# One stream of 64 KiB rows for the key, value and weight tiles of the first attention layer's groups 0 to 5

## The chip, the cores and the metric

The kernel runs on one core of a Trainium2 chip. The metric is the device time of one launch in microseconds (us); less is better. A profile of one execution by the hardware profiler stands beside the times.

## What is computed

One token passes through two layers, each an attention over a cached sequence and then a dense block; both layers use the same weights and the same cache. D is 512, there are 32 heads of 128, 4096 cached keys and a hidden width of 1376. All is float32.

```python
def _A_ref(x, k_cache, v_cache, wq, wo):
    q = (x @ wq).reshape(B, Sq, H, Dh).transpose(0, 2, 1, 3)
    scores = einsum("bhqd,bhkd->bhqk", q, k_cache) * (Dh ** -0.5)
    o = einsum("bhqk,bhkd->bhqd", softmax(scores), v_cache)
    return o.transpose(0, 2, 1, 3).reshape(B, Sq, H * Dh) @ wo

def _B_ref(x, w1, b1, w2, b2):
    return gelu(x @ w1 + b1) @ w2 + b2

for _ in range(2):
    x = x + _A_ref(_layernorm(x), ...)
    x = x + _B_ref(_layernorm(x), ...)
```

The key and value caches are 67 MB each and are read twice.

## The kernel before

The 32 heads are worked on as 8 groups (G) of 4. A group has a K tile and a V tile of 128 partitions x 64 KiB (8.39 MB, `BLOCK`), each made of 8 chunks (`NC`, 1.05 MB, 8 KiB per partition; one chunk holds 512 keys of four heads), and the group's parts of `wq` and `wo`, one chunk each. Layer 0 takes the groups in the order 0 to 7, layer 1 from 7 to 0. All tiles lie in one large tile, `arena`; SyncE issues every load on its one queue (L87, `load`), in program order, and holds an issue until the place it writes has been read by everyone.

In groups 0 to 5 of layer 0 the K tile and the V tile are loaded whole, each in one transfer, into a ring of three places of 64 KiB (`k_home`, `v_home`). The group's `wo` chunk and the next group's `wq` chunk come as a pair in one transfer of 16 KiB rows into a place of their own (`PAIR`). The order on the queue is K, V, pair, next K, and so on.

A group runs like this. `scores` (L232) multiplies each K chunk with the query on TensorE, 8 matmul records a chunk. `softmax` makes the weights `pt`. In a group with `pairs` the V chunks are weighted in place, four by ScalarE (`weighted_by_act`, L269, 16 instructions a chunk) and four by VectorE (`weighted`, L274); `add_pair` (L279) adds two neighbouring chunks to two others, three times, and one last addition (L572) adds the two that are left. With `PAIRS[0]` = (0, 2, 4, 6) the first sum is into chunks 0 and 1. After the first `add_pair`, `queries` (L213 to L223) makes the next group's query from `wq` on VectorE and one TensorE matmul (L217), with the second `add_pair` between; the third and the last addition follow. `sum_over_keys` (L283, TensorE) of the one chunk left, `scaled_out` (L287 to L292) and `summed_wo` (L309, L311), the product with `wo`, are held back (`late_sum`, `late_out`) and run within the next group's scores, after chunk 4.

Group 6 uses matmuls for its V tile (`values`, L262), group 7 gets its tiles in smaller transfers, and then the dense block and layer 1 follow.

Of the kernel before, what the change touches and what calls it, by code (L numbers as in the profile page):

```python
# [14 lines left out]
ALU = mybir.AluOpType  # L15
AX = mybir.AxisListType

P = 128
# [3 lines left out]
G = 8  # L22
J = 4
C = 8
# [3 lines left out]
U = 512  # L28
KEPT = 6

NC = 4 * U
BLOCK = 8 * NC
# [13 lines left out]
PITCH = 1024  # L46
# [7 lines left out]
LAST_IDLE = {3: 1, 5: 1, 6: 1}  # L54
WHOLE, HALVES = ((0, 8),), ((0, 4), (4, 8))
VAR_AT = 1
PAIRS = (0, 2, 4, 6), ((4, 6, 0, 2), (2, 0, 4, 6))


@with_exitstack  # L60
def decode_layers(ctx: ExitStack, tc: tile.TileContext, k, v, w, w1, w2, out):
    nc = tc.nc
    const = ctx.enter_context(tc.tile_pool(name="const", bufs=1))
    work = ctx.enter_context(tc.tile_pool(name="work", bufs=1))
# [20 lines left out]
    def load(at, src):  # L85
        t = arena[:, at : at + src.shape[-1]]
        tc.keep_in_program_order(nc.sync.dma_start(t, src))  # L87
        return t

    def pin(ins):  # L90
        tc.keep_in_program_order(ins)

    def chunk(t, i=0):
        return t[:, NC * i : NC * (i + 1)].rearrange("p (j n) -> p j n", j=4)
# [35 lines left out]
    row, _ = wq_at(0)  # L130
# [11 lines left out]
    pS, pO, pB = (psum.tile([P, 512], F32, name=n) for n in ("pS", "pO", "pB"))  # L142
# [68 lines left out]
    def queries(n, xc, wt, at, t=None, short=False, between=None):  # L211
        t = wt[:, 0, :] if t is None else t
        pin(nc.vector.tensor_scalar(t, wt[:, 0, :], xc[:, 0:1], None, op0=ALU.mult))  # L213
        for c in range(1, 4):
            pin(nc.vector.scalar_tensor_tensor(t, wt[:, c, :], xc[:, c : c + 1], t, op0=ALU.mult, op1=ALU.add))  # L215
        if short:
            pin(nc.tensor.matmul(at, one.to_broadcast([P, P]), t, start=True, stop=True))  # L217
            if between is not None:
                between()
            own = t.rearrange("p (j d) -> p j d", j=J)  # L220
            pin(nc.vector.tensor_tensor(own, at.rearrange("p (j d) -> p j d", j=J),
                                        ident[:, None, :].to_broadcast([P, J, P]), op=ALU.mult))
            pin(nc.vector.tensor_reduce(zq[:, :, C - 1], own, axis=AX.X, op=ALU.add))  # L223
            return zq
        for j in range(J):
            nc.tensor.matmul(at[:, j : j + 1], t[:, P * j : P * (j + 1)], one, start=True, stop=True)
        nc.vector.tensor_copy(zq[:, :, C - 1], at[:, :J])
        return zq
# [36 lines left out]
    def weighted_by_act(pt, t, c):  # L265
        for b in range(4):
            for j in range(J):
                own = by_head(t)[:, j, b]
                nc.scalar.activation(own, own, AF.Copy, scale=pt[:, j, c, b : b + 1])  # L269

    def weighted(pt, t, c):
        own = t.rearrange("p b (j d) -> p b j d", j=J)
        weight = pt[:, :, c, :].rearrange("p j b -> p b j")[:, :, :, None].to_broadcast([P, 4, J, DH])
        nc.vector.tensor_tensor(own, own, weight, op=ALU.mult)  # L274

    def add_pair(at, to, by):

# [3 lines left out]
    def sum_over_keys(t):  # L281
        for j in range(J):
            pin(nc.tensor.matmul(pO[32 * j : 32 * j + 4, :], one.to_broadcast([P, 4]), by_head(t)[:, j],  # L283
                                 start=True, stop=True))

    def scaled_out(rl, ot):
        nc.vector.transpose(ot[:, :512], pO)  # L287
        diag = ot.rearrange("p (b q) -> p b q", q=129)[:, :, :P]
        diag = diag.rearrange("p b (d q) -> p d b q", q=32)[:, :, :, 0]
        o, on = small("o", 4), small("on", 4)  # L290
        nc.vector.tensor_reduce(o, diag, axis=AX.X, op=ALU.add)
        nc.vector.tensor_scalar(on, o, rl, None, op0=ALU.mult)  # L292
        return on
# [14 lines left out]
    def summed_wo(on, wt, t):  # L308
        pin(nc.vector.tensor_scalar(t, wt[:, 0, :], on[:, 0:1], None, op0=ALU.mult))  # L309
        for d in range(1, 4):  # L310
            pin(nc.vector.scalar_tensor_tensor(t, wt[:, d, :], on[:, d : d + 1], t, op0=ALU.mult, op1=ALU.add))  # L311
        return t

    def add_out(t, n):
        pin(nc.tensor.matmul(pB[0:1, :], one, t, start=n == 0, stop=n == G - 2))  # L315
# [104 lines left out]
    xs, s = set_x(ahead[:, X_AT : X_AT + 4], 0.0, ahead[:, X_AT : X_AT + 4])  # L420
    nc.gpsimd.tensor_copy(b1c, ahead[:, B1_AT : B1_AT + FB])
    nc.gpsimd.tensor_copy(b2c, ahead[:, B2_AT : B2_AT + 4])
    here = {}

    def stream(what, g, pieces, base):

        for a, b in pieces:
            t = load(base + NC * a, part(k if what == "k" else v, g, a, b))
            for c in range(a, b):
                here[what, g, c] = chunk(t, c - a)  # L430
                yield c, here[what, g, c]

    w1_t = arena[:, HELD:PAIR]
    w2_t = [[arena[:, at : at + U] for at in homes] for homes in W2_AT]

# [3 lines left out]
    for layer in range(2):  # L439
        order = list(range(G)) if layer == 0 else list(range(G))[::-1]  # L440
        if layer == 0:
            nm, ss, xc = mean_of(xs, s, pN[:, 0:1], True)
            z = queries(0, xc, wq_first, pO)
        else:
            for c in range(4):
                query_block(c, xs, wq_first)
                if c == 1:
                    nm, ss, xc = mean_of(xs, s, pN[:, 0:1])
        if layer == 1:
# [5 lines left out]
            z = first_queries(negm)  # L455
        xc_l = small("xc_l", 4)
        r = rstd_of(ss, pN[:, 1:2], True)
# [4 lines left out]
        late = None  # L462
        for n, g in enumerate(order):
            first, final = n == 0, n == G - 1
            pairs = None
            if layer == 0 and n < G - 2:
                pairs = PAIRS[0]
            if layer == 1 and 1 < n < G - 2:
                pairs = PAIRS[1][n % 2]

            k_home, v_home = ((2 * n + i) % 3 * BLOCK for i in (1, 2))
            if layer == 1:
                k_home, v_home = K2_HOME if n == 2 else 15 * NC, 6 * NC * (n % 2)

            if layer == 1 and n == 0:
                tiles = [(c, here["k", g, c]) for c in range(C)]
            elif layer == 1 and n == 1:
                tiles = [(c, here["k", g, c]) for c in range(2)]
                tiles += list(stream("k", g, ((2, 3), (3, 4), (4, 8)), -2 * NC))
                n_kept = STAY + U * KEPT  # L480
                load(V1_HOME[6] + n_kept % NC, v[g][:, n_kept:BLOCK])
                for u in range(STAY, n_kept - U, U):
                    nc.scalar.copy(v_next(u), pK[(u - STAY) // U])
                for c in range(STAY // NC, C):
                    here["v", g, c] = chunk(arena[:, V1_HOME[c] : V1_HOME[c] + NC])
            elif layer == 1 and n == 2:
                tiles = [(c, here["k", g, c]) for c in range(6)]
                tiles += list(stream("k", g, ((6, 8),), 2 * BLOCK - 6 * NC))
            else:
                tiles = stream("k", g, HALVES if final else WHOLE, k_home)  # L490
            for c, t in tiles:
                scores(z, c, t)
                if late is not None and c == 4:
                    late[0]()
            held = late is not None
            if held:
                late[1]()
                late = None
# [3 lines left out]
            p, ot = free_now(layer, n)  # L502
            if layer == 1 and first:
                z = queries(n + 1, xc_l, wq_next, pO)
                nc.scalar.copy(v_next(STAY + U * KEPT - U), pB)
            pt, rl = softmax(sc, nsc, p, held)
# [3 lines left out]
            if layer == 1 and n == 0:  # L510
                for c in range(C):
                    values(c, pt, here["v", g, c], c)
            elif layer == 1 and n == 1:
                for c in range(C):
                    values(c, pt, here["v", g, c], c)

                for _ in stream("k", order[2], ((0, 6),), K2_HOME):
                    pass
            elif final:
                last_v = chunk(arena[:, v_home + BLOCK - NC : v_home + BLOCK])  # L520
                for _ in range(FILL - 2 + layer):
                    idle(t, pS)
                for c, t in stream("v", g, LAST, v_home):
                    values(c, pt, t, c, C - 1)
                    if c == C - 2:
                        others = scaled_out(rl, ot)
                    for _ in range(LAST_IDLE.get(c, 0)):
                        idle(t, pS)
                for a, b in END_PARTS[layer]:
                    at = BLOCK - NC + U * a  # L530
                    load(v_home + at, v[g][:, at : BLOCK - NC + U * b])
                for c in range(C):
                    here["v", g, c] = chunk(arena[:, v_home + NC * c : v_home + NC * (c + 1)])
            else:
                for c, t in stream("v", g, WHOLE, v_home):
                    for i in range(KEPT - 1):
                        if layer == 0 and n == G - 2 and c == (STAY + U * i) // NC:
                            nc.scalar.copy(pK[i], t[:, STAY // U % J + i - J * (c - STAY // NC), :])
                    if pairs is None:
                        values(c, pt, t, c)  # L540
# [23 lines left out]
            else:  # L564
                t = load(PAIR, of_w(wo_at(g) if layer == 0 else wq_at(g - 1), 2))
                wo_t, wq_next = (chunk(t, i) for i in ((0, 1) if layer == 0 else (1, 0)))
            if pairs:
# [6 lines left out]
                def late_sum(rl=rl, ot=ot, wt=wo_t, total=total):  # L574
                    sum_over_keys(total)
                    summed_wo(scaled_out(rl, ot), wt, ot[:, :U])

                def late_out(ot=ot, n=n):
                    add_out(ot[:, :U], n)
# [106 lines left out]
```

## Time and profile before

| what | us |
|---|---|
| median of 3 runs | 673.24 (673.19 to 673.25) |
| the profiled execution | 673.77 |
| its span, first to last instruction | 672.0 |
| VectorE busy | 406.7 |
| TensorE matmul busy | 301.1 |
| ScalarE busy | 215.4 |

The span has 6011 instructions, and 285.36 MB were moved at 425 GB/s on the mean. Busy times of different engines overlap. K0 stands for the K tile of group 0, V0 for its V tile, and so on. A DMA record is counted where a packet ends, so a window of few microseconds can show a DMA share above 1.

### The profile page before, as it was taken

The page shows a single profiled execution, that of the slowest core. Times are in us where ns is not written, and L with a number is a line of the kernel's source. Part 1 is how long each engine was busy: PE and PEld are TensorE (multiplying, and loading weights), DVE is VectorE, ACT ScalarE, POOL GpSimd, SP SyncE. Part 2 cuts the span into 40 slices and gives each one's busy share as a digit, 9 for nine tenths or more (in the row PEclk, how much of TensorE's full clock was granted, in tenths as well). Part 3 has the DMA queues.
Part 4 walks back from the last instruction along what each step waited for, and adds up shares of the span by engine and source line. Part 5 has one row for each costly group of instructions (what it writes and reads, how often), then busy time and mean ns, then how long its engine had stood idle before and what let it go on. Part 6 is the DMA issues. An engine that isn't in the chain of part 4 may idle for free.

```text
span 672.0 us, 6011 instructions
## 1 busy us (share of the span) xinstructions
PE 301.1 (45%) x2236; PEld 79.4 (12%) x2236; DVE 406.7 (61%) x510; ACT 215.4 (32%) x697; POOL 5.2 (1%) x26
## 2 busy tenths in 40 slices
PE   1501603416016053166698985604316026065597
PEld 1100100101001010011124311101001001011124
DVE  3059679497795876971422313289597794982513
ACT  0047064190560823801011200073290650910010
POOL 1000000000000000000000000000000000000000
PEclk9965855856758557586699998755757758566799
DMA  9999999999999999999999999999999999999997
GB/s 384 429 437 437 438 433 437 410 458 433 437 437 402 466 418 430 421 437 422 429 413 398 391 434 449 426 433 437 421 434 425 433 430 415 456 429 418 429 416 301
DMA packets 11548, 285.36 MB, mean 425 GB/s; under 512 B 1280, under 2 KB 1408, under 8 KB 3840
## 3 DMA queue, kind: packets, MB, share of 16 engines
q1 hardware_dynamic: 11520, 284.99, 99.1%
q8 instruction: 17, 0.28, 0.2%
q14 instruction: 11, 0.09, 0.0%
HBM read 284.92 MB, written 0.07 MB: 424 GB/s over the span
## 4 chain that ended last, share of the span: by engine, by line
DMA 65%; PE 16%; DVE 15%; issue 1%; another core or an unknown queue 1%; SPq 0%; ACT 0%; DVEq 0%; ACTq 0%
DMA arena<-in_v 38%; DMA arena<-in_k 19%; DMA arena<-in_w 8%; PE pS L232 7%; DVE arena L274 7%; PE pO L262 5%; DVE arena L279 3%; DVE arena L311 2%; DVE arena L287 1%; PE pO L283 1%; DVE arena L215 1%; PE pB L323 1%; SPq L87 0%; DVE arena L309 0%
## 5 line engine op out<-in xcount | busy, mean ns | idle before, releaser
L269 ACT ACTIVATE arena<-arena,pt 128x128 f32<-128x128 f32 x640 | 188.0, 387 | 49.1 <-DMA arena<-in_v 45.3
L232 PE MATMUL pS<-arena,smalls 128*8 128x512 f32 x1024 | 147.3, 728 | 78.6 <-DMA arena<-in_k 74.5
L279 DVE TENSOR_TENSOR arena<-arena 128x4096 f32<-128x4096 f32 x30 | 132.6, 4420 | 0.3
L217 PE MATMUL pS<-arena,smalls 128*128 128x512 f32 x20 | 20.7, 1140 | 203.4 <-DVE arena L215 203.4
L274 DVE TENSOR_TENSOR arena<-arena,pt 128x2048 f32<-128x2048 f32 x40 | 89.0, 2286 | 37.3 <-DMA arena<-in_v 34.6
L244 ACT ACTIVATE arena<-pS,smalls 128x512 f32<-128x512 f32 x16 | 12.4, 777 | 292.8 <-DVE smalls L243 292.8
L287 DVE STREAM_TRANSPOSE arena<-pO 128x512 f32<-128x512 f32 x16 | 11.5, 717 | 98.3 <-PE pO L262 60.9
L232 PEld LDWEIGHTS pS<-arena,smalls 128*8 128x8 f32 x1024 | 29.8, 102 | 199.1 <-issue 178.6
L262 PE MATMUL pO<-arena,pt 128*4 128x512 f32 x368 | 46.8, 653 | 10.8 <-DMA arena<-in_v 10.0
L236 DVE TENSOR_REDUCE smalls<-pS 128x1 f32<-128x512 f32 x16 | 11.0, 687 | 62.7 <-PE pS L232 62.7
L215 DVE SCALAR_TENSOR_TENSOR arena<-arena,smalls 128x512 f32<-128x512 f32 x45 | 33.8, 752 | 1.6
L311 DVE SCALAR_TENSOR_TENSOR arena<-arena,smalls 128x512 f32<-128x512 f32 x39 | 29.3, 752 | 1.4
L217 PEld LDWEIGHTS pS<-arena,smalls 128*128 128x128 f32 x20 | 5.0, 312 | 206.1 <-DVE arena L215 206.1
L315 PE MATMUL pB<-arena,smalls 128*1 128x512 f32 x26 | 14.1, 625 | 29.8 <-DVE arena L311 29.8
L246 PE MATMUL pO<-ident,arena 128*128 128x128 f32 x64 | 12.2, 320 | 25.6 <-ACT arena L244 25.2
L572 DVE TENSOR_TENSOR arena<-arena 128x2048 f32<-128x2048 f32 x10 | 22.9, 2292 | 0.3
L262 PEld LDWEIGHTS pO<-arena,pt 128*4 128x4 f32 x368 | 10.0, 92 | 44.4 <-issue 37.5
L382 ACT ACTIVATE smalls<-smalls 128x4 f32<-128x4 f32 (+1 forms) x6 | 1.2, 205 | 42.6 <-DVE smalls L375 24.7
L250 DVE STREAM_TRANSPOSE smalls<-smalls 128x32 f32<-128x32 f32 x16 | 3.4, 212 | 17.5 <-ACT arena L244 17.5
L437 PE MATMUL pS<-arena,ident 128*8 128x512 f32 (+1 forms) x30 | 12.9, 522 | 0.5 <-DVE pt L367 0.5
L244 ACT ACT_TABLE_LOAD x1 | 1.3, 1283 | 35.9 <-DVE smalls L243 35.9
L246 PEld LDWEIGHTS pO<-ident,arena 128*128 128x128 f32 x64 | 7.6, 155 | 39.5 <-ACT arena L244 34.1
(115 smaller groups left out, 186.2 us busy)
## 6 DMA issues: line engine op xcount, KB each, us to landing
arena<-in_w SPq DMA_DIRECT2D x13, 2048.0 KB, 12.5
arena<-in_k SPq DMA_DIRECT2D x5, 4096.0 KB, 22.3
arena<-in_v SPq DMA_DIRECT2D x2, 4096.0 KB, 32.8
arena<-in_w SPq DMA_DIRECT2D x6, 1024.0 KB, 30.7
arena<-in_k SPq DMA_DIRECT2D x1, 6144.0 KB, 21.0
arena<-in_v SPq DMA_DIRECT2D x2, 2048.0 KB, 37.3
arena<-in_w SPq DMA_DIRECT2D x7, 512.0 KB, 11.4
arena<-in_v SPq DMA_DIRECT2D x3, 1024.0 KB, 47.3
```

The source lines that it names most:

```text
L215: pin(nc.vector.scalar_tensor_tensor(t, wt[:, c, :], xc[:, c : c + 1], t, op0=ALU.mult, op1=ALU.add))
L217: pin(nc.tensor.matmul(at, one.to_broadcast([P, P]), t, start=True, stop=True))
L232: pin(nc.tensor.matmul(pS[32 * j : 32 * j + C, :], z[:, j, C - 1 - c : 2 * C - 1 - c], kt[:, j, :], start=(c == 0), stop=(c == C - 1)))
L246: nc.tensor.transpose(pT[:, b].rearrange("p j r -> p (j r)"), p[:, P * b : P * (b + 1)], ident)
L262: nc.tensor.matmul(pO[32 * j : 32 * j + 4, :], pt[:, j, c, :], by_head(vt)[:, j], start=(i == 0), stop=(i == of - 1))
L269: nc.scalar.activation(own, own, AF.Copy, scale=pt[:, j, c, b : b + 1])
L274: nc.vector.tensor_tensor(own, own, weight, op=ALU.mult)
L279: pin(nc.vector.tensor_tensor(a, a, b, op=ALU.add))
L287: nc.vector.transpose(ot[:, :512], pO)
L311: pin(nc.vector.scalar_tensor_tensor(t, wt[:, d, :], on[:, d : d + 1], t, op0=ALU.mult, op1=ALU.add))
L315: pin(nc.tensor.matmul(pB[0:1, :], one, t, start=n == 0, stop=n == G - 2))
L572: pin(nc.vector.tensor_tensor(total, total, other, op=ALU.add))
```

## The change

For groups 0 to 5 of layer 0 (and K and `wo` up to group 6) the host lays all chunks in the order of use: K chunks, the preceding group's `wo`, V chunks, the next group's `wq`. This list of 116 units is cut into row 0 with 4 units and rows 1 to 14 with 8. Each row is one transfer of 64 KiB per partition (row 0: 32 KiB) into one of three places of the ring (`flow`), and row r+3 is issued when the program has passed the last use of every unit of row r (`done`); the issue itself waits for those uses to end. Rows 0, 1 and 2 are issued at the start. The place of the pair is not used before group 6.

So rows and groups are not aligned: row 5 holds K2's chunks 1 to 7 and wo1, row 6 all of V2, row 7 wq3 and K3's chunks 0 to 6, row 8 K3's chunk 7, wo2 and V3's chunks 0 to 5, row 10 K4's chunks 5 to 7, wo3 and V4's chunks 0 to 3, row 12 K5's chunks 3 to 7, wo4 and V5's chunks 0 and 1, row 14 K6's chunks 1 to 7 and wo5.

V is worked on by one of four written plans, by n mod 4. A plan lists the chunks that ScalarE weights and VectorE's steps in order: `w5` weights chunk 5, `a40` adds chunks 0 and 1 to chunks 4 and 5, `q` begins the queries (their matmul goes off), `r` ends them, and what stands between runs beside the matmul; `s4` adds chunk 5 to chunk 4, the chunk that is summed over keys. `LATE` is the chunk of the next group's scores behind which the held-back work runs.

```diff
+EARLY = 6
+ROWS = []
+for _n in range(EARLY + 1):
+    ROWS += [("k", _n, c) for c in range(C)] + [("wo", _n - 1, 0)] * (_n > 0)
+    if _n < EARLY:
+        ROWS += [("v", _n, c) for c in range(C)] + [("wq", _n + 1, 0)]
+ROWS = [ROWS[:4]] + [ROWS[a : a + 8] for a in range(4, len(ROWS), 8)]
+PLANS = (
+    ((3, 6, 7), "w0 w1 w2 a02 w4 w5 a40 q a46 r s4"),
+    ((0, 5, 6, 7), "w1 w2 w3 a20 q w4 r a24 a26 s2"),
+    ((4, 5, 6), "w0 w1 w2 w3 a02 w7 a04 q a06 r s0"),
+    ((3, 4, 6), "w0 w1 w2 a02 w5 a04 w7 a60 q s6 r"),
+)
+LATE = 4, 6, 4, 4
...
+    def early_values(n, pt, xc):
+        by_act, plan = PLANS[n % 4]
+        for c in by_act:
+            weighted_by_act(pt, here["v", n, c], c)
+        steps = plan.split()
+        def step(s):
+            c = int(s[1])
+            if s[0] == "w":
+                pin(weighted(pt, here["v", n, c], c))
+            elif s[0] == "a":
+                by = int(s[2])
+                add_to(two(n, c), two(n, by))
+                done(("v", n, by), ("v", n, by + 1))
+            else:
+                add_to(here["v", n, c], here["v", n, c + 1])
+                done(("v", n, c + 1))
+        a, b = steps.index("q"), steps.index("r")
+        for s in steps[:a]:
+            step(s)
+        z = queries(n + 1, xc, here["wq", n + 1, 0], pS, short=True,
+                    between=lambda: [step(s) for s in steps[a + 1 : b]])
+        done(("wq", n + 1, 0))
+        for s in steps[b + 1 :]:
+            step(s)
+        return z, next(int(s[1]) for s in steps if s[0] == "s")
...
+    def flow():
+        while len(loaded) < len(ROWS) and (len(loaded) < 3 or used.issuperset(ROWS[len(loaded) - 3])):
+            r = len(loaded)
+            loaded.append(load((r + 2) % 3 * BLOCK, rows_of[r][:, : NC * len(ROWS[r])]))
+            for i, unit in enumerate(ROWS[r]):
+                here[unit] = chunk(loaded[r], i)
+
+    def done(*units):
+        used.update(units)
+        flow()
...
+            if layer == 0 and n <= EARLY:
+                flow()
+                tiles = ((c, here["k", g, c]) for c in range(C))
...
             for c, t in tiles:
                 scores(z, c, t)
-                if late is not None and c == 4:
+                if layer == 0 and n <= EARLY:
+                    done(("k", n, c))
+                if late is not None and c == (4 if layer else LATE[(n - 1) % 4]):
                     late[0]()
...
+            elif early:
+                z, first_total = early_values(n, pt, xc_l)
+                total = here["v", g, first_total]
+
+                def late_sum(rl=rl, ot=ot, n=n, total=total, first_total=first_total):
+                    sum_over_keys(total)
+                    done(("v", n, first_total))
+                    if ("wo", n, 0) not in here:
+                        flow()
+                    summed_wo(scaled_out(rl, ot), here["wo", n, 0], ot[:, :U])
+                    done(("wo", n, 0))
...
+    rows_of = np.zeros((len(ROWS), P, BLOCK + PITCH), np.float32)
```

Layer 1, and groups 6 and 7 of layer 0 from V6 on, keep their code.

## Rows read from the trace of the kernel before

**Rows 1.** DMA queues on the page: packets, MB, share of 16 engines' span.
```profile
q1 hardware_dynamic: 11520, 284.99, 99.1%
q8 instruction: 17, 0.28, 0.2%
```

**Rows 2.** Windows: us, busy per engine, PEclk, DMA share, GB/s; one group of layer 0.
```profile
113.40:157.10 43.70, 13.95 (x80) 3.15 (x80) 34.62 (x33) 19.67 (x66) 0.00 (x0) 0.62 1.00 432
```

**Rows 3.** Timeline: start, us, instruction; first use of each tile landed, layer 0.
```profile
24.95 9.13 PE L232 MATMUL pS<-arena,smalls 128*8 128x512 f32 x64 [12.57 <-DMA arena<-in_k]
...
44.37 8.90 DVE L274 TENSOR_TENSOR arena<-arena,pt 128x2048 f32<-128x2048 f32 x4 [5.01 <-DMA arena<-in_v]
...
69.33 6.56 PE L232 MATMUL pS<-arena,smalls 128*8 128x512 f32 x40 [6.72 <-DMA arena<-in_k]
...
89.25 8.90 DVE L274 TENSOR_TENSOR arena<-arena,pt 128x2048 f32<-128x2048 f32 x4 [4.48 <-DMA arena<-in_v]
...
220.23 2.29 DVE L274 TENSOR_TENSOR arena<-arena,pt 128x2048 f32<-128x2048 f32 x1 [3.30 <-DMA arena<-in_v]
...
245.20 2.75 PE L232 MATMUL pS<-arena,smalls 128*8 128x512 f32 x12 [6.73 <-DMA arena<-in_k]
...
264.54 2.29 DVE L274 TENSOR_TENSOR arena<-arena,pt 128x2048 f32<-128x2048 f32 x1 [3.27 <-DMA arena<-in_v]
...
288.84 3.46 PE L232 MATMUL pS<-arena,smalls 128*8 128x512 f32 x16 [6.06 <-DMA arena<-in_k]
```

**Rows 4.** Timeline of SyncE's queue: two issues of loads.
```profile
11.62 0.33 SPq L87 DMA_DIRECT2D arena<-in_v  x1
...
80.98 0.33 SPq L87 DMA_DIRECT2D arena<-in_w  x1
```

**Rows 5.** Chain of waits, its start: us from span's start, us, what.
```profile
0.72 4.82 DMA arena<-in_w
```

**Rows 6.** Windows of 0.1 us about the first load's first and last packets.
```profile
1.70:1.80 0.10, 0.00 (x0) 0.00 (x0) 0.10 (x1) 0.00 (x0) 0.00 (x0) 1.00 3.31 591
5.10:5.20 0.10, 0.00 (x0) 0.00 (x0) 0.00 (x0) 0.00 (x0) 0.00 (x0) 1.00 3.03 1311
```

**Rows 7.** Timeline of group 2 and the start of group 3, layer 0.
```profile
132.94 18.80 ACT L269 ACTIVATE arena<-arena,pt 128x128 f32<-128x128 f32 x64 [5.20 <-DMA arena<-in_v]
132.95 8.90 DVE L274 TENSOR_TENSOR arena<-arena,pt 128x2048 f32<-128x2048 f32 x4 [3.97 <-DMA arena<-in_v]
141.88 4.42 DVE L279 TENSOR_TENSOR arena<-arena 128x4096 f32<-128x4096 f32 x1
...
149.12 2.08 PE L217 MATMUL pS<-arena,smalls 128*128 128x512 f32 x2 [20.54 <-DVE arena L215]
...
154.03 0.69 DVE L223 TENSOR_REDUCE smalls<-arena 128x4 f32<-128x512 f32 x1
...
157.28 6.96 PE L232 MATMUL pS<-arena,smalls 128*8 128x512 f32 x40 [6.08 <-DMA arena<-in_k]
...
164.06 1.04 PE L283 MATMUL pO<-arena,smalls 128*4 128x512 f32 x8
...
166.93 2.33 DVE L311 SCALAR_TENSOR_TENSOR arena<-arena,smalls 128x512 f32<-128x512 f32 x3
...
172.63 0.25 DVE L248 COPY pt<-pO 128x128 f32<-128x128 f32 x1
```

**Rows 8.** Timeline of TensorE's weight loads, scores of group 3.
```profile
161.50 0.17 PEld L232 LDWEIGHTS pS<-arena,smalls 128*8 128x8 f32 x4 [0.69 <-issue]
162.34 0.11 PEld L232 LDWEIGHTS pS<-arena,smalls 128*8 128x8 f32 x4 [0.67 <-issue]
162.77 0.10 PEld L232 LDWEIGHTS pS<-arena,smalls 128*8 128x8 f32 x4 [0.32 <-issue]
```

**Rows 9.** Windows of 1 us in the scores of group 3 (granted clock: third last).
```profile
161.20:162.20 1.00, 1.00 (x8) 0.17 (x4) 0.18 (x1) 0.00 (x0) 0.00 (x0) 0.50 1.21 524
163.20:164.20 1.00, 1.00 (x16) 0.31 (x12) 0.00 (x0) 0.00 (x0) 0.00 (x0) 1.00 0.45 197
```

More of the change, by code (lines that the diff above doesn't have):

```diff
@@ L56, with decode_layers @@
 VAR_AT = 1
-PAIRS = (0, 2, 4, 6), ((4, 6, 0, 2), (2, 0, 4, 6))
+PAIRS = (4, 6, 0, 2), (2, 0, 4, 6)
+EARLY = 6
[5 more added lines that the diff above has]
+ROWS = [ROWS[:4]] + [ROWS[a : a + 8] for a in range(4, len(ROWS), 8)]
+assert len(ROWS[-1]) == 8
+PLANS = (
[4 rows of a table added]
+)
+LATE = 4, 6, 4, 4
 @with_exitstack
-def decode_layers(ctx: ExitStack, tc: tile.TileContext, k, v, w, w1, w2, out):
+def decode_layers(ctx: ExitStack, tc: tile.TileContext, rows_of, k, v, w, w1, w2, out):
     nc = tc.nc
@@ L273, in weighted, with add_to, two @@
         weight = pt[:, :, c, :].rearrange("p j b -> p b j")[:, :, :, None].to_broadcast([P, 4, J, DH])
-        nc.vector.tensor_tensor(own, own, weight, op=ALU.mult)
+        return nc.vector.tensor_tensor(own, own, weight, op=ALU.mult)
+    def add_to(t, by):
+        pin(nc.vector.tensor_tensor(t, t, by, op=ALU.add))
+    def two(n, c):
+        row = next(r for r in range(len(ROWS)) if ("v", n, c) in ROWS[r])
+        i = ROWS[row].index(("v", n, c))
+        assert ROWS[row][i + 1] == ("v", n, c + 1)
+        return loaded[row][:, NC * i : NC * (i + 2)]
+    def early_values(n, pt, xc):
[23 more added lines that the diff above has]
+        return z, next(int(s[1]) for s in steps if s[0] == "s")
     def add_pair(at, to, by):
@@ L431, in stream @@
                 yield c, here[what, g, c]
+    used, loaded = set(), []
+    def flow():
[7 more added lines that the diff above has]
+        flow()
     w1_t = arena[:, HELD:PAIR]
@@ L465, in decode_layers @@
             pairs = None
-            if layer == 0 and n < G - 2:
-                pairs = PAIRS[0]
             if layer == 1 and 1 < n < G - 2:
-                pairs = PAIRS[1][n % 2]
+                pairs = PAIRS[n % 2]
+            early = layer == 0 and n < EARLY
             k_home, v_home = ((2 * n + i) % 3 * BLOCK for i in (1, 2))
@@ L473, in decode_layers @@
                 k_home, v_home = K2_HOME if n == 2 else 15 * NC, 6 * NC * (n % 2)
-            if layer == 1 and n == 0:
+            if layer == 0 and n <= EARLY:
+                flow()
+                tiles = ((c, here["k", g, c]) for c in range(C))
+            elif layer == 1 and n == 0:
                 tiles = [(c, here["k", g, c]) for c in range(C)]
@@ L518, in decode_layers, with late_out @@
                     pass
+            elif early:
[8 more added lines that the diff above has]
+                    done(("wo", n, 0))
+                def late_out(ot=ot, n=n):
+                    add_out(ot[:, :U], n)
+                late = late_sum, late_out
+                continue
             elif final:
@@ L672 @@
     )
+    parts = dict(k=lambda n, c: arrays["k"][n][:, NC * c : NC * (c + 1)],
+                 v=lambda n, c: arrays["v"][n][:, NC * c : NC * (c + 1)],
+                 wq=lambda n, c: wq[n], wo=lambda n, c: wo[n])
+    rows_of = np.zeros((len(ROWS), P, BLOCK + PITCH), np.float32)
+    for r, units in enumerate(ROWS):
+        for i, (what, n, c) in enumerate(units):
+            rows_of[r, :, NC * i : NC * (i + 1)] = parts[what](n, c)
     for name in ("k", "v", "w"):
         arrays[name] = np.pad(arrays[name], ((0, 0), (0, 0), (0, PITCH)))
+    arrays = dict(rows=rows_of, **arrays)
     nc = bacc.Bacc("TRN2", target_bir_lowering=False, num_devices=1, dynamic_dma_scratch_size=64)
```

## The prediction

> **What bounds the kernel now.** I read the page's list of DMA queues first. One queue, the loads, keeps the 16 DMA engines at work for 99.1% of the span [rows 1]. Then the windows by stretch: a group in the middle of layer 0 runs at 432 GB/s with a DMA share of 1.00, while VectorE is busy for 34.6 of 43.7 us [rows 2]. So the loads set the pace and the engines wait. Third, the timeline around the first instruction that uses each landed tile [rows 3]. The reader should take differences. From K to V one 8.39 MB tile passes: 19.4 us (24.95 to 44.37, 245.20 to 264.54). From V to the next K a K tile and a 2.10 MB pair of weights pass: 24.3 us (132.95 to 157.28 [rows 7], 264.54 to 288.84). Three intervals are longer: V0 to K1 24.96, K1 to V1 19.92, V4 to K5 24.97; together 1.85 us over the usual. What lies between is regular: V1 to V2 takes 43.70 us (24.3 + 19.4), and K3 to V4 takes 62.95 (157.28 to 220.23, against 19.4 + 24.3 + 19.4 = 63.1).
>
> Is the queue ever empty? The next three loads (wo and wq, K, V) are issued together, and this begins at 80.98 for group 1 [rows 4], while V1 lands at 89.2 [rows 3]. Some 8 us of work still lay in the queue. With the share of 1.00 this says that the queue doesn't run dry in layer 0, so no wait is there to be removed.
>
> **The change part by part.**
>
> *The rows.* The bytes stay the same: K0 to K6, V0 to V5 and six pairs are 121.6 MB before; 4 units of 1.05 MB and 14 rows of 8.39 MB are 121.6 MB after. Nineteen loads become fifteen. What did a pair in 16 KiB rows cost? 24.3 - 19.4 = 4.9 us, against a quarter of a 19.4 us tile, 4.85. So 16 KiB rows are as quick per byte as 64 KiB rows, and putting the weights into 64 KiB rows brings 0.05 us a pair, 0.3 us for six. My reading of each interval is good to 0.1 us, so the bounds are -0.9 and +0.3 us. I take 0.
>
> The Trainium skill weighs against this. "DMA: Bandwidth & Descriptors", section "Anatomy of one DMA", fits each transfer (on GpSimd's path; here SyncE issues) with some 2.0 us beside its bytes, and "Rules for kernel authors" there advises to join small transfers into larger ones. By that rule four loads fewer would be an estimated 8 us; by the rows the four are worth nothing, since in a full queue the fixed part lies beside the transfer ahead.
>
> *The start.* The first load (1.08 MB) lands at 5.54 us [rows 5], and 19.4 us later K0 is there, before and after, only split: row 0 lands at 5.5 + 9.7 = 15.2 and every row r at 15.2 + 19.4 r. Row 14, which completes K6, is due at 286.8 us. By the same rule K6 was due at 286.8 us before, and came at 288.7 with the 1.85 us of the long intervals. V0 no longer waits for the first queries (it was issued at 11.62 us [rows 4]), but K0 was in transit until 24.9, so that is worth 0.
>
> *The long intervals.* They are 0.5 to 0.7 us each. The profile's page lists 17 loads of instructions, 0.28 MB in all, on a queue of their own [rows 1]: 16 KB each. At 432/16 = 27 GB/s one of them holds an engine for an estimated 0.6 us. The program's instruction count on TensorE stays, so I leave them in: 0, with bounds -1.9 (none falls badly) and +1.9 (twice as many do).
>
> *The compute.* Per group VectorE weighs 5, 4, 5, 5, 5, 4 chunks instead of 4 each, ScalarE 3, 4, 3, 3, 3, 4 instead of 4. Off the path this is free. But row r+3 goes where row r was, and SP can issue it only when every unit of row r has been used. The queue stays full if that happens within 2 x 19.4 = 38.8 us of row r's landing, less a lead of 1.4: the first load was issued at 0.72 and its first packets ended in 1.70 to 1.80; its last ended by 5.20 and it was seen as landed at 5.54 [rows 5, 6]. So 37.4 us are allowed. The steps, from group 2 to 3 of the trace [rows 7]: four weighted chunks 8.93 (132.95 to 141.88), one 2.25; a pair addition 4.4; queries on VectorE 2.8 (141.88 + 4.42 to 149.12), their matmul 2.08 beside an addition, and 1.4 after it for two reductions of 0.69 to the new query (it is ready at 154.72); five chunks of scores 6.8 (157.28 to 164.06), sum over keys 1.0; from there to the next weights 7.8 (165.10 to 172.88), of which 2.8 need wo (2.33 and a first product of some 0.5).
>
> The tightest row is row 6, which holds all of V2. Plan 2 gives w0 to w3 8.9, a02 4.4, w7 2.25, a04 4.4, q 2.8, a06 4.4 (the matmul beside it), query 1.4: 28.6. Then scores 6.8 and the sum that frees chunk 0, 1.0: 36.4 us. ScalarE's three chunks take 14.1 (18.80 for four) and lie beside. So 1.0 us is left. Next is row 10: row 8 with wo2 lands at 170.4, the weights of group 3 are ready at 170.4 + 2.8 + 3.7 = 176.9, plan 3 makes the next query in 6.7 + 4.4 + 2.25 + 4.4 + 2.25 + 4.4 + 2.8 + 2.3 + 1.4 = 30.9, and 6.8 + 1.0 + 7.8 later, at 223.4, the weights of group 4 are there; w0 to w2, a02, w4, w5, a40 take 20.0. Row 10 is free at 243.4, row 12 lands at 248.0: 3.2 us left after the lead. The other rows come out at 5 us or more. So the stream is just fed: 0, with bounds of 0 and +5.8 us (the second rival).
>
> *After the stream.* V6 goes where row 12 was, free near 280 by the same sums, needed by 286.8; then the pair for group 6 into its own place, K7 when V5's sum is made, near 298, needed when the pair has landed at 311. All are in time.
>
> **Sum.** 0 + 0 + 0 + 0: the profiled execution took 673.77 us (span 672.0 and 1.77 around it), and the change leaves it. The median of the runs is 673.24, 0.53 less; I shift the forecast to it and, as the unknown terms reach further up than down, write 673.3.
>
> **Rivals.**
>
> *Nothing late and no long intervals.* Two of the three long ones, V0 to K1 and V4 to K5, contain a separate weight load, as all V-to-K intervals do; with the weights inside the rows and fewer loads, the strays may go. For it: a stray is no part of the bytes, since the other four V-to-K intervals with the same content have none. Against it: those four have a weight load too, and the third long interval has none. Price: -1.85, so 671.4 us.
>
> *The ring starves.* Plans 2, 3 and 0 need 28.6, 30.9 and 28.6 us to the query and 15.6 more to the next weights: 44.2, 46.5 and 44.2 us a group, against 43.7 for the loads. Before, one pair addition stood ahead of the query products (141.88); now two do in plans 0 and 2 and three in plan 3. The compute chain becomes the bound if it is over 1.0 us longer than I reckon by row 6. For it: the score matmuls start on an idle TensorE at the granted 0.50 (1.2 GHz), four in 0.84 us, and at 1.00 (2.4 GHz) four take 0.43 [rows 8, 9]; should all 40 run at the lower level, 8.4 us stand for 6.8. That alone makes row 9 late by 0.6 us. With 3 us more per group, row 9 is 2.0 us late, and row 13 by 9 - 2.0 - 3.2 = 3.8 more: 5.8. Against it: in the trace the clock rose after 5 us of scores in this very place (157.28 to 162.34). I price it at 2.5, so 675.7 us.
>
> *The fixed cost of a transfer.* Were it paid in the stream, the part of a load that isn't bytes would fall away four times. From a row: the first load took 4.82 us [rows 5] for 1.08 MB, 2.5 us at the stream's rate, so 2.3 us are beside the bytes; four of these make 9.2, and 664 us. By the intervals [rows 3, 7] a load of weights costs 0.05 us beside its bytes. That rule is the one of the Trainium skill named above; the trace doesn't agree with it here.
>
> **How the numbers follow.** A measurement can tell 0.2%, 1.35 us, from no change. The forecast of no change 0.50; strays gone 0.22; ring starved 0.25; the fixed cost 0.03. Faster is 0.22 + 0.03 = 0.25, slower 0.25. The range reaches to both rivals: from 670.9 to 676.3 us, the lower end at the strays' price and the 0.3 us of the rows, and a little more, the upper a little over the second rival's middle price; past it lie the longest chains and the third rival. The forecast's own range is 672.0 to 674.6.
>
> **What would show it.** In the changed profile row r's first use should come at 15.2 + 19.4 r, and the issue of row 9, behind the sum over keys of group 2, about 1 to 3 us before row 8 lands; the DMA share should be 1.00 in every group. A share under 0.97 around 170 or 248 us, with SP waiting there for TensorE's sum or VectorE's addition, shows starvation. Rows spaced by less than 19.3 us on average would show that 64 KiB rows or fewer loads are quicker after all, and make me wrong on the fast side.

## The result, and the profile after

| | median us | runs | ratio to before (95%) |
|---|---|---|---|
| before | 673.26 | 7 | |
| changed | 676.07 | 7 | 1.0036 (1.0024 to 1.0048) |

The change makes the kernel 0.36% slower, 2.4 us by the ratio and 2.8 by the medians; the forecast of no change (673.3, with a range of its own from 672.0 to 674.6) missed, and the time lies near the upper end of the range that reaches to the rivals (670.9 to 676.3). The profiled execution took 676.07 us against 673.77. All of this arises in the stream: V6 lands at 310.14 us against 308.05, and from there to the end the spans take 364.1 and 363.9 us.

The page first: the bytes and the 17 loads of instructions on q8 are those of [rows 1], with 576 packets fewer. A second queue of instruction loads, q14, has 10 for 11 before; its loads are of 8 KB.

```profile
span 674.3 us, 5950 instructions
...
q1 hardware_dynamic: 10944, 284.99, 99.0%
q8 instruction: 17, 0.28, 0.2%
q14 instruction: 10, 0.08, 0.0%
```

Next the windows, one for each step from one row's landing to the next (us, busy time of PE, PEld, DVE, ACT, POOL with counts, granted clock, DMA share, GB/s). A row of 8.39 MB should take 19.4 us at 432 GB/s, as in [rows 2]. Rows 6, 10 and 12 do, within 0.1; rows 13 and 14 take 20.5 and 20.7, and in row 13's step the DMA share is 0.95.

```profile
113.60:133.00 19.40, 11.04 (x70) 2.43 (x70) 13.45 (x21) 0.87 (x2) 0.00 (x0) 0.76 1.01 437
191.00:210.40 19.40, 2.71 (x6) 0.62 (x10) 18.36 (x11) 4.78 (x16) 0.00 (x0) 0.50 1.00 432
230.00:249.50 19.50, 0.83 (x1) 0.50 (x2) 19.25 (x11) 9.90 (x34) 0.00 (x0) 0.50 1.04 431
249.50:270.00 20.50, 13.53 (x80) 2.56 (x78) 13.03 (x21) 0.87 (x2) 0.00 (x0) 0.75 0.95 409
270.00:290.70 20.70, 3.97 (x10) 0.62 (x10) 20.45 (x14) 18.80 (x64) 0.00 (x0) 0.50 1.03 444
```

The timeline of group 2 and 3 answers [rows 7] step by step. V2 is used from 133.06, the query is ready at 161.37 (28.3 us; I had 28.6), the scores' first five chunks take 5.66 (I had 6.8: the granted clock was 0.50 up to 163.4 us and 1.00 from 164.4 on, so it rose some 3 us after the scores began; before, it rose after 5), the sum over keys ends at 168.12.

```profile
133.06 8.90 DVE L290 TENSOR_TENSOR arena<-arena,pt 128x2048 f32<-128x2048 f32 x4 [2.92 <-DMA arena<-in_rows]
141.99 4.42 DVE L293 TENSOR_TENSOR arena<-arena 128x4096 f32<-128x4096 f32 x1
146.33 2.29 DVE L290 TENSOR_TENSOR arena<-arena,pt 128x2048 f32<-128x2048 f32 x1
...
160.68 0.69 DVE L239 TENSOR_REDUCE smalls<-arena 128x4 f32<-128x512 f32 x1
...
161.43 5.84 PE L248 MATMUL pS<-arena,smalls 128*8 128x512 f32 x40 [3.59 <-DVE smalls L239]
...
167.09 1.03 PE L337 MATMUL pO<-arena,smalls 128*4 128x512 f32 x8
```

Last SyncE's queue, with the issues of rows 9, 11 and 13, each right behind the last use of a place:

```profile
168.24 0.33 SPq L103 DMA_DIRECT2D arena<-in_rows  x1
...
203.44 0.33 SPq L103 DMA_DIRECT2D arena<-in_rows  x1
...
246.01 0.33 SPq L103 DMA_DIRECT2D arena<-in_rows  x1
```

Row 9 left at 168.24, 35.3 us after row 6's landing at 132.94, inside the 37.4 us that the prediction allowed. Row 13 left at 246.01, 35.6 us after row 10's landing at 210.39. The DMA view gives row 13's time from issue to landing, 24.0 us, so it landed at 270.0, 20.5 us after row 12.

```profile
arena<-in_rows SPq DMA_DIRECT2D x1, 24.0
```

The landing alone does not show that the 16 DMA engines report 16 separate ends for every load. These times were read from the trace's completion records (first engine, eighth, last, which is the landing):

```
load               first    8th      last
before  V1         87.42    87.68    89.16
        K6        286.18   286.50   288.70
        V6        305.53   305.86   308.05
changed row 3      72.94    73.15    73.42
        row 4      92.36    92.56    94.21
        row 8     169.75   169.94   171.66
        row 9     189.55   190.19   191.03
        row 12    247.62   248.27   249.48
        row 13    268.02   268.91   270.02
        row 14    287.40   288.28   290.76
        V6        306.75   307.64   310.14
```

The reader should compare the steps of the columns with 19.37. Row 9: the first engine took 19.80, the eighth 20.25, the last 19.37. So the loss was on the faster engines, and the landing didn't show it. Row 13: all three took 20.4 to 20.6. Row 4 and row 14: the first took 19.4, the last 20.8 and 20.7. These are two different losses, one of the whole queue and one of single engines.

### The profile page after: what moved, and what is told of

It is laid out like the page before. It is cut to its first block, busy times and chain, and to the rows that moved or that the text cites. A ratio compares the mean times of both kernels' runs of the same rounds, so it can differ in the third digit from the quotient of the medians.

```text
span 674.3 us, 5950 instructions
## 1 busy us (share of the span) xinstructions
PE 309.7 (46%) x2236; PEld 79.2 (12%) x2236; DVE 415.9 (62%) x514; ACT 197.0 (29%) x633; POOL 5.2 (1%) x26
## 4 chain that ended last, share of the span: by engine, by line
DMA 50%; DVE 32%; PE 15%; issue 2%; ACT 0%; SPq 0%; DVEq 0%; ACTq 0%
DMA arena<-in_v 27%; DMA arena<-in_rows 16%; DVE arena L290 12%; DVE arena L293 9%; DMA arena<-in_w 8%; PE pS L248 6%; PE pO L278 5%; DVE arena L333 3%; DVE arena L365 2%; DVE arena L231 1%; DVE arena L341 1%; PE pO L262 1%; DVE smalls L252 1%; PE pB L377 1%; PE pO L337 0%
## 5 line engine op out<-in xcount | busy, mean ns | idle before, releaser
L248 PE MATMUL pS<-arena,smalls 128*8 128x512 f32 x1024 | 151.3, 742 | 65.1 <-DMA arena<-in_k 24.6
L285 ACT ACTIVATE arena<-arena,pt 128x128 f32<-128x128 f32 x576 | 169.6, 387 | 33.3 <-DMA arena<-in_v 15.7
L233 PE MATMUL pS<-arena,smalls 128*128 128x512 f32 x20 | 20.8, 1141 | 209.2 <-DVE arena L231 209.2
L290 DVE TENSOR_TENSOR arena<-arena,pt 128x2048 f32<-128x2048 f32 x44 | 98.4, 2286 | 16.2 <-DMA arena<-in_v 10.6
L293 DVE TENSOR_TENSOR arena<-arena 128x4096 f32<-128x4096 f32 (+1 forms) x24 | 93.3, 3888 | 1.1
L333 DVE TENSOR_TENSOR arena<-arena 128x4096 f32<-128x4096 f32 x12 | 53.0, 4419 | 0.1
L369 PE MATMUL pB<-arena,smalls 128*1 128x512 f32 x26 | 16.1, 704 | 32.8 <-DVE arena L365 32.8
## 6 DMA issues: line engine op xcount, KB each, us to landing
arena<-in_k SPq DMA_DIRECT2D x1, 6144.0 KB, 20.4
```

Of the source, the lines that this page charges most:

```text
L248: pin(nc.tensor.matmul(pS[32 * j : 32 * j + C, :], z[:, j, C - 1 - c : 2 * C - 1 - c], kt[:, j, :], start=(c == 0), stop=(c == C - 1)))
L290: return nc.vector.tensor_tensor(own, own, weight, op=ALU.mult)
L293: pin(nc.vector.tensor_tensor(t, t, by, op=ALU.add))
L333: pin(nc.vector.tensor_tensor(a, a, b, op=ALU.add))
```

## The experiments

Three theories stood against each other. A: rows 9 and 13 are issued too late for the queue, since the written plans release the places late. B: the rows as such cost the time, by their place in HBM or their cut. C: loads of instructions hold single DMA engines. In what follows a step is the time from one load's end to the next one's, on the engine named, and "late" is what a step takes beyond an undisturbed one.

**Held-back work earlier** (ratio to before 0.9997, 0.9986 to 1.0008; 673.56 against 673.99 us).

```diff
-LATE = 4, 6, 4, 4
+LATE = 1, 6, 1, 1
```

> The held-back work of groups 0, 2 and 3 runs behind the second chunk of the next group's scores instead of the fifth (LATE 1, 6, 1, 1). Theory A, late issues: rows 9 and 13 are issued too shortly before the queue runs out (168.2 and 246.0 us, when the first engine ends the row ahead at 169.5 and 247.2), and their first packets take up to 3.9 us for 2.42. Here row 9 should be issued near 165.9 and row 13 near 244.0, the step from row 12 to 13 should fall from 20.5 us to under 19.8, and the time should be about 1.2 us below the changed kernel's 676.1, so 674.5 to 675.2 us. Theory B, the rows themselves (their place in HBM, their cut) cost the time: row 13 still takes 20.5 us and the time stays at 675.5 to 676.5. Theory C, only loads of instructions on the slowest DMA engine cost it: as B, within 1 us either way, with the steps of 20.5 us wherever those loads fall.

Rows 9 and 13 were issued 2.0 and 2.65 us earlier:

```profile
166.21 0.33 SPq L103 DMA_DIRECT2D arena<-in_rows  x1
...
243.36 0.33 SPq L103 DMA_DIRECT2D arena<-in_rows  x1
```

Row 13 landed 25.4 us behind its issue, at 268.7, and its step was 19.35 us:

```profile
arena<-in_rows SPq DMA_DIRECT2D x1, 25.4
```

In the windows the step to row 13 has the share back, 0.99 for 0.95, and row 14's is 19.5 for 20.7:

```profile
249.40:268.70 19.30, 12.33 (x78) 2.64 (x78) 13.03 (x23) 3.24 (x11) 0.00 (x0) 0.77 0.99 429
268.70:288.20 19.50, 3.97 (x10) 0.63 (x10) 19.20 (x11) 16.43 (x57) 0.00 (x0) 0.50 1.04 447
```

The run gains 2.4 us of span (671.9 for 674.3). 1.2 of it is row 13's step, as theory A forecast. The other 1.2 is no part of theory A: it is row 14's last engine, which came 0.1 us late here and 1.4 in the changed kernel, whose first and eighth engines were not late in that step.

**Held-back work later** (1.0043, 1.0028 to 1.0058; 676.72 us).

```diff
-LATE = 4, 6, 4, 4
+LATE = 6, 6, 6, 6
```

> The held-back work runs behind the seventh chunk in every group (LATE 6, 6, 6, 6). Theory A: row 9 is issued near 170 us and row 13 near 248, past the time when the first engine ends the row ahead; both rows lose 1.5 to 3 us on all engines, and the time is 678 to 681 us. Theories B and C: no change against the changed kernel, 675.5 to 676.5 us.

A miss in size: by its time this run can't be told from the changed kernel (1.0036), as theories B and C have it, and only the steps speak for theory A. Row 9 was issued at 170.77, 1.0 us after the first engine had ended row 8, and its step was 21.8 us, 2.4 too long; so far as forecast. Row 13 lost only 0.2.

```profile
170.77 0.80 SPq L103 DMA_DIRECT2D arena<-in_rows  x2
```

```profile
171.70:193.50 21.80, 3.18 (x14) 0.91 (x14) 19.88 (x22) 10.35 (x35) 0.00 (x0) 0.60 1.04 433
252.00:271.60 19.60, 11.85 (x75) 2.14 (x74) 11.06 (x16) 0.22 (x1) 0.00 (x0) 0.76 1.00 432
```

Row 9's loss had moved all later landings back, so row 13, issued at 247.35, was 2.7 us ahead of the first engine's end of row 12 at 250.03. Here the delay of one row became a lead for the next: the losses don't add up.

**V's work left out** (0.9997, 0.9988 to 1.0006; 673.68 us). The weighting and the additions of V in groups 0 to 5 of layer 0 are not computed.

```diff
-        for c in by_act:
-            weighted_by_act(pt, here["v", n, c], c)
...
             if s[0] == "w":
-                pin(weighted(pt, here["v", n, c], c))
+                pass
...
-                add_to(two(n, c), two(n, by))
                 done(("v", n, by), ("v", n, by + 1))
...
-                add_to(here["v", n, c], here["v", n, c + 1])
                 done(("v", n, c + 1))
```

> The weighting and the additions of V in groups 0 to 5 of layer 0 are left out (the sum over keys takes the one chunk as it lies), so the rows are free early and all are issued with over 8 us of work in the queue; the stream, its rows and its order stay. Theory A: row 14 lands as K6 did before, 287 to 289.5 us, and the time is 672.5 to 674.3 us. Theory B: the rows still cost 2 us or more, 675 to 676.5. Theory C: between, as the loads of instructions fall; 672.5 to 675.

Row 14 landed at 287.87 us, V6 at 307.22. Rows 10 and 13 took 19.37 and 19.35 us:

```profile
191.10:210.40 19.30, 10.31 (x50) 1.97 (x50) 5.23 (x9) 0.00 (x0) 0.00 (x0) 0.68 1.01 435
249.20:268.50 19.30, 9.98 (x54) 2.07 (x54) 6.42 (x18) 0.87 (x2) 0.00 (x0) 0.68 1.01 435
```

Theory B falls: the stream in 64 KiB rows is neither slower nor quicker than K, V and pairs. Even with all waits for V's work gone the time is that of before. Two things differ from what was expected. Row 9 was issued only 3.6 us ahead of the first engine's end of row 8, and lost nothing. And with the instructions of V's work gone, q14 has 1 load in the stream (up to 309 us) for 5, so the run takes away some of theory C's loads as well. Theory A's part is seen apart from them: no first engine was late in any step.

**The kernel before, one release delayed** (1.0025, 1.0014 to 1.0036; 675.64 us).

```diff
+DELAY = 9
...
-                    summed_wo(scaled_out(rl, ot), wt, ot[:, :U])
+                    on = scaled_out(rl, ot)
+                    if layer == 0 and n == 2:
+                        for _ in range(DELAY):
+                            pin(nc.vector.tensor_copy(ot[:, :U], ident[:, None, :].to_broadcast([P, 4, P])))
+                    summed_wo(on, wt, ot[:, :U])
```

> The kernel before, with 9 copies of 512 columns on VectorE (about 4.4 us) ahead of group 2's product with wo, so that the pair, K4 and V4 are issued near 173.7 instead of 169.3 us, when the first engine ends V3 near 174.4 and the last near 176.3. Theory A (a late issue costs with any tensor): the next landing, of the pair, comes 0.4 to 1.2 us late, and the time is 673.6 to 674.5 us. Theory B (it is the rows): nothing is late, 673.0 to 673.5. Theory C as B.

The nine copies take 4.11 us and the pair leaves at 173.59, where the first engine ended V3 at 174.66:

```profile
166.53 4.11 DVE L580 COPY arena<-ident 128x512 f32<-128x512 f32 x9
...
173.59 0.33 SPq L88 DMA_DIRECT2D arena<-in_w  x1
```

```profile
arena<-in_w SPq DMA_DIRECT2D x1, 2048.0 KB, 9.7
```

It landed at 183.30, 6.58 us after V3 where a pair takes 4.89: 1.7 us lost by one load issued 1.1 us ahead, with the old tensors. Theory A holds beyond the stream, and its price was above the 0.4 to 1.2 that I gave it. The time, 675.64, is above the forecast of 673.6 to 674.5 too; another 1.0 us came with the next pair, on its last engine alone, where the first lost nothing and an 8 KB load of instructions stands at 226.5 us.

**The plans alone** (1.0073, 1.0056 to 1.0089; 678.85 us). Whole K and V tiles and pairs as before, with the four plans and LATE.

```diff
+    def planned(n, pt, at, xc, wt):
+        by_act, plan = PLANS[n % 4]
...
-                if late is not None and c == 4:
+                if late is not None and c == (LATE[(n - 1) % 4] if layer == 0 else 4):
...
+                if layer == 0:
+                    z, first_pair = planned(n, pt, v_home, xc_l, wq_next)
```

> The kernel before with its whole K and V tiles and its pair, but with the four written plans and LATE 4, 6, 4, 4 for V in groups 0 to 5; no stream. Theory A (the plans lengthen the chain from V to the release of a place, so loads are issued too late): the pair of group 3 is issued near 173.3 us, that of group 4 near 220, when V3 and V4 are all but landed (176.5, 220.1), and they come 1 to 4 us late each; the time is 676 to 681 us. Theory B (the rows in HBM cost the time, not the order of the work): 673.2 to 674.2 us, as before.

The issues of groups 3's and 4's pairs came at 174.82 and 222.02:

```profile
174.82 0.33 SPq L94 DMA_DIRECT2D arena<-in_w  x1
...
222.02 0.33 SPq L94 DMA_DIRECT2D arena<-in_w  x1
```

```profile
arena<-in_w SPq DMA_DIRECT2D x1, 2048.0 KB, 7.2
```

The first engine had ended V4 at 220.35, so the queue was dry on it; the pair landed at 229.18, 2.1 us late, and its first engine came 3.5 us late. The plans cost the time without the stream too. The stream gives some of it back: with it the same plans cost 2.4 us, without it 4.9.

**More code** (1.0028, 1.0018 to 1.0038; 675.44 us).

```diff
+MORE = 48
...
+            if pairs and layer == 0:
+                for _ in range(MORE):
+                    pin(nc.tensor.matmul(pS[:C, :8], ident[:, :C], ident[:, :8], start=True, stop=True))
```

> The kernel before, with 48 small matmuls more (8 columns) in each of layer 0's groups 0 to 5, in TensorE's wait for V; they compute nothing that is used. It is to show what the long intervals are. Theory C (each load of instructions holds one DMA engine and the slowest engine sets the landing): the page shows 20 to 23 loads of instructions for 17, the last engine's landing of V6 falls further behind the first engine's than the 2.5 us of before (3 to 5 us), and the time is 0.4 to 2.5 us longer, 673.7 to 676 us. Rival (these loads run beside and the long intervals have another cause): no change, 673.0 to 674.0.

```profile
span 673.6 us, 7163 instructions
...
q8 instruction: 22, 0.36, 0.2%
```

Five loads of instructions more, and 1.9 us more by the ratio; V6's last engine came 3.45 us after its first (2.5 before). One is seen by itself: a load of instructions at 43.94 us, and V0's last engine ends at 46.04 where 15 others end by 44.36. No load came shortly behind the end of the queue (the leads are 5.0 us and more), the first engine lost nothing in any step, and no tensor changed.

Do such loads stand in the long intervals of [rows 3]? These are the DMA view's lines for V0 to K1 (44.3 to 69.2 us), K1 to V1 (69.2 to 89.2) and V4 to K5 (220.2 to 245.1) of the kernel before:

```profile
q14 instruction: 2, 0.02, 0.2%
...
q8 instruction: 1, 0.02, 0.3%
...
q14 instruction: 2, 0.02, 0.2%
```

So each long interval holds loads of instructions, as theory C has it, but only K1 to V1 one of the 17 of [rows 1]; the other two hold 8 KB loads on q14, a queue that the prediction didn't look at. Four more such loads (123.6, 143.9, 206.0 and 257.0 us) stand in intervals of the usual length: there the landing moved by 0.1 us at most, since another engine was the last. Up to 309 us the stream has 4 loads on q8 and 5 on q14, before and after, so C by number explains no difference between the two kernels; where they fall does differ.

## Why the prediction was right or wrong

**What bounds the kernel: right.** With V's work gone or released early the time is 673.6 to 673.7, beside 674.0 of before. No wait was there to be removed in layer 0: the queue was full.

**The rows: right.** Rows take 19.36 us for 8.39 MB in every step that nothing disturbs, and a pair in 16 KiB rows 4.89 in the kernel before; a quarter of a row is 4.84. The 0.05 us a load stands against the estimated 2 us of the Trainium skill ("DMA: Bandwidth & Descriptors", "Anatomy of one DMA"). That fit is of GpSimd's path; for SyncE's full queue the trace does not agree with it.

**The chain of work: nearly right.** Row 6 was released 35.3 us after its landing (36.4 forecast), row 10 35.6 (34.2). The groups' chains are longer than before, as forecast, and the plans alone show it.

**The lead: this step failed.** "less a lead of 1.4" counted from a row's landing and from the time of a first packet. Both were wrong. A landing is the last engine's: the first had ended row 8 at 169.75, 1.9 us before. (The records of [rows 6] stand at a packet's start, not at its end as is said ahead of the prediction, so 1.0 us after its issue the first load only begins.) And a load issued shortly ahead started slowly: the 16 first packets of row 13 took 2.6 to 4.0 us where a packet takes 2.42, even on engines that got to it 3 us after its issue. Why they were slow is not shown by any run. The leads, counted to the first engine's end of the load ahead, and the delay of the first and the last engine over the undisturbed step:

```
load                       lead us   first late   last late
plans alone, pair 4          -1.7        3.5         2.1
work later, row 9            -1.0        2.9         2.4
plans alone, pair 3           0.8        1.2         0.0
before delayed, pair 3        1.1        1.1         1.7
plans alone, pair 5           1.2        0.7         0.0
changed, row 9                1.5        0.4         0.0
changed, row 13               1.6        1.0         1.2
plans alone, pair 1           2.3        0.6         1.0
work later, row 13            2.7        0.2         0.2
plans alone, pair 2           3.6        0.2         0.0
V's work left out, row 9      3.6        0.0         0.0
work earlier, row 9           3.6        0.0         0.0
work earlier, row 13          3.9        0.0         0.0
before, pair 5                4.3        0.0         0.0
```

(In plans alone, pair 1, an 8 KB load of instructions at 93.5 us adds to the last engine's 1.0.) So from 3.6 us ahead of the first engine on hardly anything was lost (0.2 at most), at 2.7 and less something each time. Ahead of the landing that is 3.6 + 1.9 = 5.5 us, and 38.8 - 5.5 = 33.3 us are allowed, not 37.4. By this rows 6 (36.4) and 10 (34.2) were released late by the prediction's own sums, and the direction would have come out right. The sign that the prediction named came true for row 13, with a share of 0.95 and SyncE waiting for VectorE's addition, and not for row 9.

The second rival's price, 675.7, was met, by another way than it says and in part by luck: row 10's chain was 1.4 us longer than reckoned, but the allowance was 4.1 us shorter, and 1.1 us of the loss are loads of instructions.

**The long intervals: left in, and that was right; their price was too low and where they fall was not forecast.** The prediction put a load of 16 KB at an estimated 0.6 us of an engine's time. In the packets' records it is 1.4 to 1.6: 0.9 to 1.1 for the load, and 0.5 by which that engine's next packet takes longer than its 2.42 us. The 8 KB loads of q14, which it left out, hold an engine for 0.6 to 1.0 us. The last engine lost 2.0 us to them from K0 to K6 before. In the changed profile it lost 4.3 us over its 14 steps, of which 1.2 is row 13's late issue and 3.1 are such intervals (rows 4, 11, 12, 14). The changed kernel's runs spread from 675.0 to 676.8. That the loads of instructions fell worse by 1.1 in the profiled execution is read from it: in row 4's step stand one load on q8 and two on q14, in row 14's one and one. Why they fall there and on these engines was not tried, and the other executions were not profiled. The Trainium skill ("DMA: Bandwidth & Descriptors", "Why a DMA increments its semaphore by 16 and not by 1") says that a load has landed when all its engines have reported. The trace agrees: the 16 ends of V6 spread over 2.5 us before.

**The first rival** (strays gone) was wrong: the long intervals hold loads of code, and the stream has as many after as before. **The third** (fixed cost saved) was wrong by the 0.05 us above.

## What to carry to other kernels

In a kernel like this one, whose loads never stop, reordering the work gained nothing and a longer chain from landing to release cost time. Compute each buffer's release against the queue, from the first engine's end of the load ahead and not from the landing, and keep some 4 us between. Where a ring is tight, look first for a release that can be moved, here the sum over keys from the fifth chunk to the second. In a queue that stays full, joining loads was worth some 0.05 us a load.

## What was not expected of the hardware

A load of instructions holds one DMA engine, for 1.4 to 1.6 us at 16 KB and 0.6 to 1.0 at 8 KB, and in these traces that engine stays behind for the rest of the stream: in the kernel before the last engine is 1.8 us behind the first from V1 on and 2.5 us from K5 on. The landing of every later load is late by this, while the other engines have a lead that shows nowhere but in the completion records. No version tried beats the kernel before; the best, with the work held back less, equals it.
